# A transformer block with Fourier mixing on one core: row copies from two queues, sums on VectorE, and a new order of outputs and loads

## The chip, the core and the metric

The kernel runs on one core of a Trainium2 chip. The core has five engines with instruction queues of their own: TensorE (PE) for matmuls, VectorE (DVE), ScalarE (ACT) and GpSimd (POOL) for elementwise work, and SyncE (SP), which here only starts transfers. Transfers go through the core's 16 DMA engines; those that SP starts run in a hardware queue (q1 in the profile), those that POOL starts in a software queue (q0). An engine takes its instructions in order, so an instruction that waits holds up everything behind it on the same engine; this is true of SP and POOL when they wait before starting a transfer.

The metric is the device time of one execution in microseconds. The runs of one kernel are compared by their median. Beside it there is one profiled execution, with every instruction's start and length, from which the views below come.

## The reference

```python
y   = x + FNet(x) + MLP(layernorm(x))        # x: 1 x 2048 x 640
# FNet: y = Cs @ (x @ Ch) - Ss @ (x @ Sh), with the DFT matrices of the
#       hidden axis (640 x 640) and of the sequence axis (2048 x 2048)
# MLP:  gelu(h @ w1 + b1) @ w2 + b2, w1: 640 x 1536, w2: 1536 x 640
```

This is its content in short form: a real part of a two-dimensional Fourier transform and a two-layer perceptron on the normalized rows, both added to x. All of it is float32.

## The kernel before

Every float32 product is made of three matmuls of a reduced 32-bit type: high part by high part, high by low, low by high (`product`, L300 to L302; `hidden` has the same in one line, L320). `split` makes the parts: the high part on ACT (L186), the low part on VectorE (L189). One such triple with a 128 x 128 weight and 512 columns is the unit of PE's work.

The 2048 rows are four token blocks of 512 (block 0 to 3), the 1536 hidden columns twelve chunks of 128, and the 640 columns five blocks of 128. The work on PE stands in this order:

- 0 to 92 us: the MLP of block 0. The loop over i splits chunks of w1 and w2 (`prep_w1`, `prep_w2`), starts loads of later chunks (`load_w1`, `load_w2`, on SP), runs `background(i)`, then `hidden(i + 2)` (15 matmuls of L320), `gelu`, `late(i)` and `output(i)` (15 matmuls of L300 to L302). Behind it, `background` and `late` prepare the rows of blocks 1 and 2: layernorm (`ln_scale`, `ln_apply`, L231), then `put_z` and `put_rows`.
- 92 to 211 us: `pair(k)`, k = 0 to 5: blocks 1 and 2 together, two hidden chunks of both at a time, by sums and differences (forms) of their rows, in the manner of Strassen's method. A `window` is a run of products into one bank. In it `term`, `unit` and `split_unit` take the banks over to ACT and VectorE (L340, L463), `put_out(n)` takes n entries off the list `outputs` and runs them as output products, and `beside_pair(k, at)` runs side work at a fixed place: the sums of block 0 (`finish`), the weights of the hidden-axis transform (`turn_w`, `prep_w`), loads.
- 211 to 262 us: the loop over p with the late outputs of block 2. `load_unit(i)` brings a unit back from `gs` in DRAM on SP, `split_unit` splits it, and `between(p)` prepares block 3: layernorm, `put_z`, `put_rows`, transposes, weights, the sums of block 1.
- 262 to 341 us: the MLP of block 3, with the start of the sequence transform's inputs behind it; 342 to 862 us: the sequence transform.

`put_z` (L735) re-lays a block's normalized rows within SBUF, so that a partition holds other rows: 16 copies of 80 KB. It is called for block 2 (`z_b`, from tile r, in `late(1)`), block 1 (into the tile `row`, from `rt`, in `background(3)`; the view names it `row<-rt`), and block 3 (`z<-row`, in `between(3)`). All 48 are started by POOL. `put_rows` (L743) stores the same rows to `xn` in DRAM in four copies of 320 KB; POOL starts them, but for block 2, where SP does, in `background(2)`.

From z the forms are made (`make_forms`): a transpose on VectorE (L259), the high part on ACT (L186), the low part on VectorE (L189). On ACT and VectorE they stand in order with the splits of the weight chunks and the gelus of the loop over i: `make_forms("b", ...)` in `background(4)` and `make_forms("a", ...)` in `background(5)` come in one turn, the split of the chunk for the next `hidden` only in the following turn. `as` and `r` are names of tiles for the parts of w1 and w2.

`finish(t, *es)` takes column block e of the second MLP product of block t out of its bank: ACT adds the bias (L382), VectorE transposes (L384, tile `ot`), and an addition puts it onto x (L386, tile `xo`). That addition runs on POOL for blocks 0 and 2 and on VectorE for block 1. `turn_sum` is the same without the addition. `store_sums` (L918) stores the sums from POOL to `ys` in DRAM. For block 2 the column blocks come as (3), (4, 0) beside the last gelu, and (1, 2) behind it. The build of the sequence transform's sums takes over the place of block 2's `xo`, so its first instruction waits for those stores.

Of the kernel before, what the change touches and what calls it, by code (L numbers as in the profile page):

```python
# [10 lines left out]
F32 = mybir.dt.float32  # L11
# [4 lines left out]
P = 128  # L16
Q = 4
B = 32
# [8 lines left out]
def kernel(  # L27
# [45 lines left out]
    nc = tc.nc  # L73
# [657 lines left out]
    def put_z(z, rows):  # L731

        for a in range(NC):
            for q in range(Q):
                nc.gpsimd.dma_start(  # L735
                    z[q * B : (q + 1) * B].rearrange("r (c a) d -> r a c d", a=NC)[:, a],
                    rows[a * B : (a + 1) * B, :, q * DQ : (q + 1) * DQ],
                )

    def put_rows(t, rows, eng=nc.gpsimd):  # L740

        for a in range(NC):
            eng.dma_start(  # L743
                xn[:, t * B : (t + 1) * B].rearrange("(c a) r d -> a r c d", a=NC)[a], rows[a * B : (a + 1) * B]
            )

    def background(i):

        if i == 0:
            for c in range(NC):  # L750
                ln_apply(c)
            put_rows(0, row_places)
            A["rows_a"] = rows_in("rt2")
            for c in range(NC, 2 * NC):
                load_x(c, home=A["rows_a"])
            ln_stats(8)
            ln_stats(9)
        if i == 2:
            put_rows(2, A["rows_b"], nc.sync)
            ln_stats(4)  # L760
            ln_stats(5)
        if i == 3:
            ln_scale(NC)
            Z["a"] = as_z(row_places)
            for c in range(NC, 2 * NC):
                ln_apply(c)
            put_z(Z["a"], A["rows_a"])
            put_rows(1, A["rows_a"])
        if i == 4:
# [12 lines left out]
        if i == 7:  # L782
            open_place(*PLACES[8])
            make_forms("b", "t10", "t11")
            add(vb, vb, ub, ALU.subtract)
        if i == 8:
            turn_x("t20", "b")
            turn_x("t21", "b")
            add(ua, vb, ua, ALU.subtract)
            add(va, va, vb, ALU.subtract)  # L790
            load_xo(0)

    def late(i):

        if i == 0:
            ln_stats(10)
            ln_stats(11)
        if i == 1:
            ln_scale(NC)
            Z["b"] = zo_tile("z_b")  # L800
            for c in range(2 * NC, 3 * NC):
                ln_apply(c)
            put_z(Z["b"], A["rows_b"])
        if i == 2:
            ln_stats(6)
            ln_stats(7)
# [94 lines left out]
    def keep(g, a):  # L901
        nc.gpsimd.dma_start(gs[g % NF], a)

    def finish(t, *es, home=None, eng=nc.gpsimd):

        for e in es:
            add_block(xo[t], e, oacc[t][e], f"ot{t}_{e}", eng, bias=b2c[:, e : e + 1], **(home or {}))

    def turn_sum(t, e):
        nc.scalar.activation(oacc[t][e], oacc[t][e], AF.Identity, bias=b2c[:, e : e + 1])  # L910
        yt = mr.tile([P, TB], F32, tag="ab", bufs=2, name=f"ot{t}_{e}")
        nc.vector.transpose(yt, oacc[t][e])
        return yt

    def store_sums(t, *ks):
        for k in ks or range(len(YCOLS)):
# [7 lines left out]
    def beside_pair(k, at):  # L924
# [43 lines left out]
        if k == LASTK and at == 2:  # L968
            for i in range(3):
                load_unit(i)  # L970
        if k == LASTK and at == 4:
            for i in range(6, 8):
                load_unit(i)
            load_x(14)
            load_x(15)
            load_xo(1, place("xab2", (P, NB, DQ), F32))

    units = {}
# [7 lines left out]
    def pair(k):  # L986
# [4 lines left out]
        u = term(a1, x_)  # L991
        window(y_, "A", 2, "va", True, ("A", 4, "oa0"))
        make_pieces(k + 1, *(("Bh", "Ah") if k else ("Ah",)))
        beside_pair(k, 2)
        put_out(0 if k else 5)
        u = unit(a1, y_, u, u)
        make_pieces(k + 1, *(("Al", "Bl") if k else ("Al",)))
        window(z_, "D", 2, "t1", True, (b, 2, "ob0"))
        zc = mr.tile([P, TB], F32, tag="zt", bufs=2, name=f"zc{k}") if k else early.tile([P, TB], F32, tag="w2r", bufs=3, name="zc0")
# [26 lines left out]
        if not k:  # L1026
            make_pieces(1, "Dh", "Dl", "Ch", "Cl")
        beside_pair(k, 4)
        outputs.extend((g, e) for g in (a1, a2) for e in range(ND))

    def between(p):

        if p == 0:
            ln_stats(12)
            ln_stats(13)
        if p == 1:
            held = [turn_sum(1, e) for e in (3, 4)]
            A["held"] = held
            ln_stats(14)
        if p == 2:  # L1040
            ln_stats(15)
        if p == 3:
            ln_scale(NC)
            Z["z"] = zo_tile("z3")
            for c in range(3 * NC, 4 * NC):
                ln_apply(c)
            put_z(Z["z"], row_places)
            put_rows(3, row_places)
            new_xt(3)
        if p == 4:  # L1050
            for e, yt in zip((3, 4), A["held"]):
                d = xo[1][:, :, e * B : (e + 1) * B]
                add(d, d, yt.rearrange("p (n i) -> p n i", i=B))
        if 4 <= p < 7:
            finish(1, p - 4, home=in_zt, eng=nc.vector)
        for j in {7: (0,), 8: (1, 2), 9: (3, 4)}.get(p, ()):
            if j == 0:
                transpose_z("x30", Z["z"], 0)
            if j + 1 < ND:
                transpose_z(f"x3{j + 1}", Z["z"], j + 1)  # L1060
            prep_xt(f"x3{j}", j)
        if p == 9:
            load_xo(2)
        if p == 10:
            store_sums(1)
        if p == 11:
            open_place(*PLACES[3])
        if p == 12:
            open_place(*PLACES[2])
        for n in {0: (0,), 4: (1,), 5: (2,), 6: (3,), 7: (4,), 8: (5,), 9: (6,), 10: (7,), 11: (8,), 12: (9, 10), 13: (11,)}.get(p, ()):  # L1070
            prep_w1(AGAIN[n], 2 * NF + n)
            load_w1(2 * NF + 3 + n)

    def fourier_step(i):
        if 2 <= i < 2 + 2 * NK:
# [48 lines left out]
    for p in range(2 + NF):  # L1124
        g = 2 * NF - 2 + p
        if p == NF:
            output(g)
            gelu(g + 2, hidden(g + 2))
        elif p == NF + 1:
            acc = hidden(g + 2)  # L1130
            output(g)

            def fill(k):
                finish(2, *((3,), (4, 0))[k])

            gelu(g + 2, acc, fill)
            finish(2, 1, 2, home=in_zt)
            store_sums(2)
        else:
            output(g, (3, 4, 0, 1, 2) if p == 1 else range(ND))  # L1140
            split_unit(g + 2, units[p])
            if p in (0, 1, 2, 8):
                load_unit(min(8 + p, NF - 1))
        between(p)


# [538 lines left out]
```

## Time and profile before

| | |
|---|---|
| median of 3 runs | 864.52 us (863.22 to 866.62) |
| profiled execution | 864.51 us |
| its span, first to last instruction | 862.5 us |
| mean granted clock of TensorE | 0.998 |
| PE busy | 846.3 us (98%) |
| VectorE busy | 686.9 us (80%) |
| ScalarE busy | 366.7 us (43%) |
| POOL busy | 87.2 us (10%) |
| DMA moved | 166.52 MB, mean 193 GB/s |

Busy time of PE is from the start of a matmul to its modelled end, and matmuls overlap, so 98% leaves open how far PE is from its peak; the count of matmuls in a stretch tells that. In a row of the timeline the first number is the start, the second the length of the group, then engine, line, operation, output and inputs, the count, and in brackets the idle time before the group and what ended it. A DMA row of POOL or SP (`SPq`) is the starting of a transfer, not its flight. A window row gives, for each engine, busy time and the count of instructions, then the granted clock (1.00 is full), the busy share of the DMA engines and what they moved.

### The profile page before, as it was taken

What the parts mean: (1) busy time and instruction counts of PE and PEld (TensorE: products, weight loads), DVE (VectorE), ACT (ScalarE), POOL (GpSimd) and SP (SyncE); (2) the same over time, 40 slices, a digit from 0 to 9 for tenths busy, and PEclk for the clock granted to TensorE, in tenths of its full rate; (3) what the DMA queues carried; (4) which work ended last, traced back from release to release, by engine and by line L of the source; (5) the groups of instructions that cost most, each with busy time, mean ns of one, the idle gap of its engine ahead of it and who ended that gap; (6) DMA issues with size and microseconds to landing.
All of it is one profiled execution on the core that took longest, in us unless ns stands there. A gap on an engine that the chain in (4) does not pass through costs nothing.

```text
span 862.5 us, 10569 instructions
## 1 busy us (share of the span) xinstructions
PE 846.3 (98%) x3711; PEld 696.1 (81%) x3711; DVE 686.9 (80%) x897; ACT 366.7 (43%) x528; POOL 87.2 (10%) x138
## 2 busy tenths in 40 slices
PE   8999999999999999999999999999999999999997
PEld 6877877888877888788888888888888888888885
DVE  6868887875865578988988787998977998886687
ACT  6636565665444456344434333332322422223241
POOL 0360043333334000000000000000000000000000
PEclk9999999999999999999999999999999999999999
DMA  8895546878997893959663659854665879804464
GB/s 231 243 262 158 120 119 205 258 234 289 263 250 182 271 401 92 218 115 231 150 168 87 169 152 313 206 105 129 166 178 178 252 183 231 319 18 177 122 169 106
DMA packets 201252, 166.52 MB, mean 193 GB/s; under 512 B 65744, under 2 KB 172496, under 8 KB 200688
## 3 DMA queue, kind: packets, MB, share of 16 engines
q1 hardware_dynamic: 187552, 138.20, 60.5%
q0 software_dynamic: 8368, 26.75, 9.3%
q10 hardware_dynamic: 5280, 0.92, 0.6%
q8 instruction: 29, 0.48, 0.2%
q14 instruction: 23, 0.19, 0.1%
HBM read 115.75 MB, written 46.14 MB: 188 GB/s over the span
## 4 chain that ended last, share of the span: by engine, by line
PE 74%; DMA 11%; DVE 6%; ACT 3%; SPq 2%; issue 2%; POOL 1%; POOLq 0%; DVEq 0%; ACTq 0%
PE banks L300 24%; PE banks L301 24%; PE banks L302 24%; PE banks L320 3%; DMA w1r<-in_B_w_dram 2%; DMA row<-xn 2%; DMA z_b<-r 2%; DMA xab<-in_A_x_dram 1%; DMA ys<-xo 1%; SPq L278 1%; DVE xab L463 1%; DMA row<-rt 1%; DVE sums L463 1%; POOL xo L386 1%; DVE w1f L189 1%
## 5 line engine op out<-in xcount | busy, mean ns | idle before, releaser
L301 PE MATMUL banks<-as,xab 128*128 128x512 f32 x407 | 158.4, 389 | 0.3 <-DVE as L189 0.3
L186 ACT ACTIVATE as<-r 128x1024 fp32r<-128x1024 f32 x80 | 85.0, 1062 | 173.3 <-PE banks L302 148.5
L300 PE MATMUL banks<-as,xab 128*128 128x512 f32 x407 | 158.3, 389 | 0.0
L302 PE MATMUL banks<-as,xab 128*128 128x512 f32 x407 | 158.3, 389 | 0.0
L189 DVE TENSOR_TENSOR as<-r,as 128x1024 fp32r<-128x1024 f32 x80 | 97.2, 1215 | 38.7 <-ACT as L186 38.7
L301 PEld LDWEIGHTS banks<-as,xab 128*128 128x128 f32 x407 | 76.4, 188 | 16.6 <-DVE as L189 0.8
L300 PEld LDWEIGHTS banks<-as,xab 128*128 128x128 f32 x407 | 76.4, 188 | 15.9
L302 PEld LDWEIGHTS banks<-as,xab 128*128 128x128 f32 x407 | 76.4, 188 | 15.8
L300 PE MATMUL banks<-as,xc 128*128 128x512 f32 x224 | 87.1, 389 | 0.0
L301 PE MATMUL banks<-as,xc 128*128 128x512 f32 x224 | 87.1, 389 | 0.0
L302 PE MATMUL banks<-as,xc 128*128 128x512 f32 x224 | 87.1, 389 | 0.0
L186 ACT ACTIVATE as<-rt 128x1024 fp32r<-128x1024 f32 x32 | 34.0, 1062 | 69.9 <-PE banks L302 57.9
L320 PE MATMUL banks<-xt,xab 128*128 128x512 f32 x240 | 56.7, 390 | 0.0
L320 PEld LDWEIGHTS banks<-xt,xab 128*128 128x128 f32 x240 | 44.9, 188 | 9.5 <-DVE xt L189 0.2
L189 DVE TENSOR_TENSOR hs<-ab,hs 128x512 fp32r<-128x512 f32 x36 | 26.3, 730 | 28.9 <-ACT hs L186 28.4
L302 PEld LDWEIGHTS banks<-as,xc 128*128 128x128 f32 x224 | 42.0, 188 | 8.8
L300 PEld LDWEIGHTS banks<-as,xc 128*128 128x128 f32 x224 | 42.0, 188 | 8.7
L301 PEld LDWEIGHTS banks<-as,xc 128*128 128x128 f32 x224 | 42.0, 188 | 8.7
L300 PE MATMUL banks<-hs,xc 128*128 128x512 f32 x120 | 46.9, 391 | 2.2 <-DVE ot L384 2.2
L301 PE MATMUL banks<-hs,xc 128*128 128x512 f32 x120 | 46.7, 389 | 0.0
L302 PE MATMUL banks<-hs,xc 128*128 128x512 f32 x120 | 46.7, 389 | 0.0
L189 DVE TENSOR_TENSOR as<-rt,as 128x1024 fp32r<-128x1024 f32 x32 | 38.8, 1211 | 5.3 <-ACT as L186 5.3
(228 smaller groups left out, 1662.3 us busy)
## 6 DMA issues: line engine op xcount, KB each, us to landing
raw<-in_A_dft_seq_re_dram SPq DMA_DIRECT2D x64, 256.0 KB, 5.7
raw<-in_A_dft_seq_im_dram SPq DMA_DIRECT2D x64, 256.0 KB, 5.4
w1r<-in_B_w_dram SPq DMA_DIRECT2D x144, 80.0 KB, 3.2
wit<-wst POOLq DMA_DIRECT2D x15, 384.0 KB, 4.0
ws<-wit SPq DMA_DIRECT2D x15, 384.0 KB, 5.5
wit<-wst POOLq DMA_DIRECT2D x20, 256.0 KB, 4.4
forms_ab<-xab SPq DMA_DIRECT2D x4, 1280.0 KB, 7.7
xab<-wit SPq DMA_DIRECT2D x13, 384.0 KB, 4.8
```

The costliest lines, as they stand in the source:

```text
L186: nc.scalar.activation(h, s, AF.Copy)
L189: nc.vector.tensor_tensor(l, s, h.bitcast(F32), op=ALU.subtract)
L278: eng.dma_start(t[q * B : (q + 1) * B], v[q, :, :, f0 : f0 + P])
L300: nc.tensor.matmul(acc, wh, mh, start=first, stop=False, skip_group_check=goes_on)
L301: nc.tensor.matmul(acc, wh, ml, start=False, stop=False, skip_group_check=goes_on)
L302: nc.tensor.matmul(acc, wl, mh, start=False, stop=last, skip_group_check=goes_on)
L320: nc.tensor.matmul(acc, W1[i][:, a, j * P : (j + 1) * P], XT[j][:, b], start=n == 0, stop=n == len(steps) - 1)
L386: eng.tensor_tensor(d, d, yt.rearrange("p (n i) -> p n i", i=B), op=ALU.add)
L463: nc.vector.tensor_tensor(dst, a, b, op=op)
```

## The change

- `put_z` starts its copies from POOL and SP in turn: q = 0 and 2 from POOL, q = 1 and 3 from SP. For each of the three blocks that is 8 and 8.
- `put_rows` is always started by POOL; for block 2 it is called in `late(1)`, right behind `put_z`, no longer in `background(2)`.
- `finish` always adds on VectorE. For block 2 the transposes and the additions are taken apart: `turn_sum` of block 3 in the first gap beside the last gelu; in the second `turn_sum` of 4, 0, 1, the addition of 3, `turn_sum` of 2; the additions of 4, 0, 1, 2 behind the gelu. Their tiles come from two pools, so that none waits for an addition.
- In `pair(k)`, `beside_pair(k, 2)` stands behind `unit(a1, ...)` and no longer ahead of it. It holds `finish(0, 2)` for k = 1 and `prep_w(0, 1)` for k = 2.
- The outputs of pair 0 come as columns 0, 1, 2 of both units, then columns 3, 4 of both.
- In the last pair, x(14) and x(15) are loaded ahead of units 6 and 7; `load_unit(11)` and `load_xo(2)` start behind the w1 load of the same turn.

The number of instructions on PE (matmuls and the rest) and on ACT is unchanged; VectorE has ten more (836 for 826), POOL nine fewer (80 for 89), SP three more (242 for 239).

```diff
@@ put_z, put_rows
-                nc.gpsimd.dma_start(
+                (nc.gpsimd, nc.sync)[q % 2].dma_start(
                     z[q * B : (q + 1) * B].rearrange("r (c a) d -> r a c d", a=NC)[:, a],
                     rows[a * B : (a + 1) * B, :, q * DQ : (q + 1) * DQ],
                 )
-    def put_rows(t, rows, eng=nc.gpsimd):
+    def put_rows(t, rows):
-            eng.dma_start(
+            nc.gpsimd.dma_start(
@@ background
         if i == 2:
-            put_rows(2, A["rows_b"], nc.sync)
@@ late
             put_z(Z["b"], A["rows_b"])
+            put_rows(2, A["rows_b"])
@@ finish, turn_sum
-    def finish(t, *es, home=None, eng=nc.gpsimd):
+    def finish(t, *es, home=None):
-            add_block(xo[t], e, oacc[t][e], f"ot{t}_{e}", eng, bias=b2c[:, e : e + 1], **(home or {}))
+            add_block(xo[t], e, oacc[t][e], f"ot{t}_{e}", nc.vector, bias=b2c[:, e : e + 1], **(home or {}))
-    def turn_sum(t, e):
+    def turn_sum(t, e, home=mr, tag="ab"):
-        yt = mr.tile([P, TB], F32, tag="ab", bufs=2, name=f"ot{t}_{e}")
+        yt = home.tile([P, TB], F32, tag=tag, bufs=2, name=f"ot{t}_{e}")
+    def add_sum(t, e, yt):
+        d = xo[t][:, :, e * B : (e + 1) * B]
+        add(d, d, yt.rearrange("p (n i) -> p n i", i=B))
@@ beside_pair
         if k == LASTK and at == 4:
+            load_x(14)
+            load_x(15)
             for i in range(6, 8):
                 load_unit(i)
-            load_x(14)
-            load_x(15)
@@ pair
-        beside_pair(k, 2)
         put_out(0 if k else 5)
         u = unit(a1, y_, u, u)
+        beside_pair(k, 2)
...
-        outputs.extend((g, e) for g in (a1, a2) for e in range(ND))
+        for es in ((0, 1, 2), (3, 4)) if k == 0 else (range(ND),):
+            outputs.extend((g, e) for g in (a1, a2) for e in es)
@@ between
-            finish(1, p - 4, home=in_zt, eng=nc.vector)
+            finish(1, p - 4, home=in_zt)
-        if p == 9:
-            load_xo(2)
...
+        if p == 8:
+            load_unit(NF - 1)
+        if p == 9:
+            load_xo(2)
@@ the late outputs of block 2
             def fill(k):
-                finish(2, *((3,), (4, 0))[k])
-
+                if k == 0:
+                    kept[3] = turn_sum(2, 3, rows, "yt")
+                else:
+                    kept[4] = turn_sum(2, 4, rows, "yt")
+                    kept[0] = turn_sum(2, 0, **in_zt)
+                    kept[1] = turn_sum(2, 1, **in_zt)
+                    add_sum(2, 3, kept[3])
+                    kept[2] = turn_sum(2, 2, rows, "yt")
             gelu(g + 2, acc, fill)
-            finish(2, 1, 2, home=in_zt)
+            for e in (4, 0, 1, 2):
+                add_sum(2, e, kept[e])
             store_sums(2)
...
-            if p in (0, 1, 2, 8):
-                load_unit(min(8 + p, NF - 1))
+            if p < 3:
+                load_unit(8 + p)
```

More of the change, by code (lines that the diff above doesn't have):

```diff
@@ L1051, in between @@
             for e, yt in zip((3, 4), A["held"]):
-                d = xo[1][:, :, e * B : (e + 1) * B]
-                add(d, d, yt.rearrange("p (n i) -> p n i", i=B))
+                add_sum(1, e, yt)
         if 4 <= p < 7:
-            finish(1, p - 4, home=in_zt, eng=nc.vector)
+            finish(1, p - 4, home=in_zt)
         for j in {7: (0,), 8: (1, 2), 9: (3, 4)}.get(p, ()):
@@ L1133, in fill @@
             def fill(k):
[L1134 removed]
+                if k == 0:
[6 more added lines that the diff above has]
+                    kept[2] = turn_sum(2, 2, rows, "yt")
+            kept = {}
             gelu(g + 2, acc, fill)
[L1137 removed]
+            for e in (4, 0, 1, 2):
+                add_sum(2, e, kept[e])
             store_sums(2)
```

## The prediction

> **What bounds the kernel now.** I read the page first, then busy time in 20-us stretches, then PE's waits, then the timelines around each wait. In the stretches the columns are the window, its length, busy time and count of PE, weight loads, VectorE (DVE), ScalarE (ACT) and GpSimd (POOL), the granted clock, the DMA share and GB/s.
>
> The page:
>
> ```profile
> span 862.5 us, 10569 instructions
> ...
> PE 846.3 (98%) x3711; PEld 696.1 (81%) x3711; DVE 686.9 (80%) x897; ACT 366.7 (43%) x528; POOL 87.2 (10%) x138
> ```
>
> The stretches:
>
> ```profile
> 40.00:60.00 20.00, 20.00 (x90) 16.57 (x89) 13.02 (x29) 6.51 (x10) 13.74 (x26) 1.00 1.04 272
> 60.00:80.00 20.00, 17.80 (x68) 13.33 (x67) 15.90 (x24) 11.06 (x19) 3.87 (x8) 0.91 0.65 187
> 120.00:140.00 20.00, 18.09 (x79) 14.33 (x78) 14.58 (x27) 10.23 (x22) 9.03 (x11) 1.00 0.67 181
> 140.00:160.00 20.00, 18.66 (x82) 14.86 (x81) 17.97 (x42) 13.39 (x30) 8.48 (x15) 1.00 0.70 232
> 200.00:220.00 20.00, 20.00 (x90) 16.57 (x89) 12.61 (x31) 9.57 (x21) 5.71 (x10) 1.00 0.85 296
> 240.00:260.00 20.00, 19.82 (x86) 15.75 (x85) 12.68 (x19) 10.01 (x16) 4.58 (x6) 1.00 0.94 247
> 260.00:280.00 20.00, 19.55 (x86) 15.83 (x85) 11.00 (x12) 9.71 (x16) 10.66 (x8) 1.00 0.71 178
> 340.00:360.00 20.00, 19.66 (x87) 15.96 (x86) 18.57 (x23) 9.92 (x15) 0.00 (x0) 1.00 1.21 223
> ```
>
> PE is busy 98% of the span. In 40:60 and 200:220 it is full: 90 matmuls in 20 us, 0.222 us each. What a stretch lacks of 20.00 can be won, not more: 2.20 us in 60:80, 1.91 in 120:140, 1.34 in 140:160, 0.18, 0.45 and 0.34 in the last three. Besides, 60:80 has a clock of 0.91, which makes busy time long. PE's own instructions stay as they are, so the change can win only there.
>
> PE's waits (in total, times, longest):
>
> ```profile
> PE banks L300 <- DVE ot L384: 2.2, 2, 1.7
> PE banks L320 <- ACT as L186: 1.9, 2, 1.6
> ...
> PE banks L300 <- ACT zc L186: 1.6, 2, 1.3
> ```
>
> PE's timeline at 60-72 us:
>
> ```profile
> 62.14 5.70 PE L320 MATMUL banks<-xt,as 128*128 128x512 f32 x15 [1.57 <-ACT as L186]
> ...
> 71.62 1.59 PE L320 MATMUL banks<-xt,as 128*128 128x512 f32 x4 [0.37 <-ACT as L186]
> ```
>
> PE's timeline in pair 1:
>
> ```profile
> 124.85 0.50 PE L300 MATMUL banks<-hs,xc 128*128 128x512 f32 x1 [1.70 <-DVE ot L384]
> ```
>
> A stretch of 2 us:
>
> ```profile
> 64.00:66.00 2.00, 2.00 (x6) 1.57 (x5) 0.00 (x0) 0.00 (x0) 1.70 (x4) 0.50 0.81 203
> ```
>
> The waits lie in those stretches. At 60–72 us PE waits 1.57 and 0.37 us for `as`, the parts of a w1 chunk. The 15 matmuls of hidden(8) from 62.14 then take 5.70 us instead of some 3.5 (14 x 0.222 and the end of the last), because the clock is 0.50 at 64:66: 2.2 us. Together the place costs 1.57 + 0.37 + 2.2 = 4.1 us; without it hidden(9) would start at 71.62 - 4.1 = 67.5.
>
> Why `as` is late: ScalarE takes its work in order, and ahead of the chunk's high part stand the forms of z.
>
> ACT's timeline:
>
> ```profile
> 66.93 1.22 ACT L186 ACTIVATE xab<-ztua 128x512 fp32r<-128x512 f32 x2 [4.21 <-DVE ztua L259]
> ...
> 70.85 0.72 ACT L186 ACTIVATE as<-w1r 128x640 fp32r<-128x640 f32 x1
> ```
>
> VectorE's timeline:
>
> ```profile
> 66.18 1.30 DVE L259 STREAM_TRANSPOSE ztua<-row 128x512 f32<-128x512 f32 x2 [2.51 <-DMA row<-rt]
> ```
>
> POOL's timeline:
>
> ```profile
> 50.91 1.64 POOL L735 DMA_DIRECT2D row<-rt  x3 [1.53 <-DMA z_b<-r]
> 53.30 1.63 POOL L735 DMA_DIRECT2D row<-rt  x3 [0.75 <-DMA z_b<-r]
> 56.24 3.80 POOL L735 DMA_DIRECT2D row<-rt  x7 [1.31 <-DMA z_b<-r]
> 60.84 0.55 POOL L735 DMA_DIRECT2D row<-rt  x1 [0.80 <-DMA row<-rt]
> 62.32 0.55 POOL L735 DMA_DIRECT2D row<-rt  x1 [0.93 <-DMA row<-rt]
> 63.10 0.55 POOL L735 DMA_DIRECT2D row<-rt  x1 [0.23 <-DMA row<-rt]
> 64.30 2.18 POOL L743 DMA_DIRECT2D xn<-rt  x4 [0.64 <-DMA row<-rt]
> ```
>
> The chain of waits:
>
> ```profile
> 63.10 2.70 DMA row<-rt
> ```
>
> POOL issues the 16 copies of the second z (row<-rt) from 50.91 to 63.65, waiting for landings of its own earlier copies. The chain of waits has the last landing at 65.8, VectorE transposes at 66.18, ScalarE makes the forms from 66.93, and only behind them `as` for hidden(9) at 70.85. So as(9) is ready 5.74 us after that landing (71.58), and hidden(9) starts at 71.62. The wait of 1.57 us before hidden(8) stands likewise behind the forms of the first z (z_b).
>
> **The change, part by part.**
>
> *Copies from two queues.* The 48 row copies (three z of 16) go alternately to POOL and SP, so 24 leave POOL. The four row stores of block 2 go from SP to POOL, behind z_b's eight there. On SP eight copies of z_b come ahead of w1(8), and eight of row<-rt ahead of w1(10) and w2(8); all wait for the layernorm's rows, so these weights wait with them. w1(8) is needed for hidden(8) near 61, some 15 us later: nothing. w1(10) comes from 54.97 to some 58–60, needed near 74: nothing, unless the second z is late. The first z need be only 1.57 us earlier for hidden(8) to run without a wait; POOL's waits on z_b's landings (1.53 + 0.75 + 1.31) alone are longer, so I let that wait and its clock drop go. But that only moves the stall: hidden(9) still needs as(9). The gain of the place is how much earlier the second z lands than 65.84, at most 4.1 us.
>
> Bounds of that landing. Below: POOL's waits for its own landings inside the 16 issues are 0.75 + 1.31 + 0.80 + 0.93 + 0.23 = 4.0 us; with two queues none remain, which gives 61.8. Above: the four block 2 stores (1280 KB) now stand on POOL's queue before row<-rt, and the four xn<-rt come beside SP's half.
>
> SP's timeline:
>
> ```profile
> 43.55 3.50 SPq L743 DMA_DIRECT2D xn<-r  x4
> ...
> 54.97 1.92 SPq L278 DMA_DIRECT2D w1r<-in_B_w_dram  x4
> ```
>
> At the 203 GB/s of 64:66 another 1280 KB in front are 6.3 us, at the 272 of 40:60 they are 4.7: the landing at 70.5 to 72.1. Against it, SP's w1 and w2 chunks that were issued from 54.97 on (w1(10), w2(8), part of w1(11), about 960 KB) now come behind row<-rt, some 3.5 us at 272 GB/s, which gives 67.0 and, with the stores early in flight, up to 70.5 as the end of the range. I take 63.0, nearer the lower end: the rows that end the landing are POOL's waits for itself, with the engines at 0.81 in 64:66, not full. This is -2.8 us, and PE waits 68.7 - 67.5 = 1.2 us there. Whether such a wait halves the clock is open: 1.57 us at 62.14 did, 1.70 us at 124.85 did not (1.00 in 120:140). I charge nothing and keep +2.2 for the range.
>
> The Trainium skill, "DMA: Bandwidth & Descriptors", section "Issuing engines are not separate DMA queues", speaks against this part: copies started from several engines end up on the same 16 DMA engines, and only the time to start them is saved. By it the landing would stay at 65.8 or later, the place would gain nothing, and the sum would be 863.5. The share of 1.04 in 40:60 agrees with it; POOL's waits at issue are the room that the rule leaves.
>
> *Additions on VectorE.* Ten additions leave POOL.
>
> The additions (line 386; min/median/max in ns):
>
> ```profile
> L386 POOL TENSOR_TENSOR xo<-xo,ot x10: 1284/1297/1868, 115.9 to 274.1; 128x512 f32<-128x512 f32 x10
> ...
> L386 DVE TENSOR_TENSOR xab<-xab,ot x3: 692/693/693, 231.7 to 237.1; 128x512 f32<-128x512 f32 x3
> ```
>
> VectorE's timeline in pair 1:
>
> ```profile
> 114.40 0.82 DVE L189 TENSOR_TENSOR w1f<-w1r,w1f 128x640 fp32r<-128x640 f32 x1
> ...
> 118.78 2.87 DVE L189 TENSOR_TENSOR w1f<-w1r,w1f 128x640 fp32r<-128x640 f32 x2
> ...
> 127.34 2.26 DVE L189 TENSOR_TENSOR w1f<-w1r,w1f 128x640 fp32r<-128x640 f32 x1
> 129.53 0.67 DVE L463 TENSOR_TENSOR zc<-zc,banks 128x512 f32<-128x512 f32 x1
> ```
>
> in pair 2:
>
> ```profile
> 151.16 0.68 DVE L463 TENSOR_TENSOR zc<-zc,banks 128x512 f32<-128x512 f32 x1
> ```
>
> On POOL one takes 1297 ns, on VectorE 693. While POOL adds, VectorE's L189 takes 2.87 us for two and 2.26 for one instead of the 0.82 of 114.40: some 2.7 us lost. The five additions of block 0 on VectorE cost 5 x 0.69 = 3.5. Nearly equal, so VectorE comes to zc (129.53) at the same time or up to 0.8 later.
>
> *finish behind the unit, outputs regrouped (pairs 1 and 2).* The wait at 124.85 (1.70 us, third output's bank held by transposition L384) goes, as finish(0,2) no longer stands before it in the way it did, and the 1.3 us for ACT zc in 140:160 goes, because prep_w(0,1) comes behind. What is late next: the window t4 needs zc, made by VectorE, which has no idle time before 129.53 in pair 1 nor before 151.16 in pair 2. PE arrives earlier and waits there instead. I take +0.3 for both, with bounds -3.2 (what 120:140 and 140:160 lack: 1.91 + 1.34) and +2.1 (three additions ahead of zc at 0.69, and none of the lost time regained).
>
> *Third z (block 3).*
>
> POOL's timeline, third z:
>
> ```profile
> 234.63 4.34 POOL L735 DMA_DIRECT2D z<-row  x8 [1.56 <-DMA z<-row]
> ```
>
> PE's timeline, late outputs:
>
> ```profile
> 272.43 0.50 PE L300 MATMUL banks<-hs,xc 128*128 128x512 f32 x1 [0.45 <-DVE ot L384]
> ```
>
> VectorE's, there:
>
> ```profile
> 270.62 1.12 DVE L189 TENSOR_TENSOR hs<-ab,hs 128x512 fp32r<-128x512 f32 x1
> ```
>
> POOL issues 8 copies, waits 1.56 us, issues 8 more; with two queues the last starts some 4 us earlier, x(14) and x(15) come earlier too. PE has 0.18 us missing in 240:260 as idle and 86 matmuls instead of 90, so -0.5, at most 4 x 0.222 = -0.9; later weights come behind the copies, which can give it back: 0 is the other end.
>
> *Block 2's sums in the last outputs.* PE's 0.45 us at 272.43 waits for a transposition, which waited for POOL's sums; VectorE's hs beside them takes 1.12. Transposes first, additions after the gelu: the wait goes, -0.5; 0 if VectorE is late. The stores of block 2 follow as much earlier and the later stretch 340:360 may regain its 0.34: -0.3.
>
> *Loads in another order.* load_unit(11) behind the w1 load, load_xo(2) behind it too, x(14), x(15) ahead of two units: nothing. The cover is PE's queue in 200:220, full; if a unit is late there, PE waits as long as it is late.
>
> Sum: -2.8 + 0.3 - 0.5 - 0.5 - 0.3 = -3.8 (all but the first: -1.0). The profiled execution took 864.51 us (862.5 of span and 2.0 around it), the median of the runs is 864.52: no correction. That gives 860.7 us.
>
> **The rivals.**
>
> *Pairs 1 and 2 gain too* (VectorE is not the bound there). For it: the named waits end on ACT and on a transposition, not on zc's row. Against: VectorE has no idle time in the rows before 129.53. It gives 860.7 - 0.3 - 3.2 = 857.2.
>
> *Bandwidth decides* (the change doesn't bring the copies earlier). For it: the engines' share in 40:60 is 1.04. Against: 0.81 in 64:66. The second z lands between 65 and 67, PE waits 3 to 5 us at 67.5 in one piece, and the clock is halved then: at 65.84 it is 864.5 + 2.2 - 1.0 = 865.7, in all 864.9 to 866.9. This is what the rule of the Trainium skill on issuing engines would bring.
>
> *Slower: the second z is held up behind the rows of block 2.* These 1280 KB stand on POOL's queue before its half of row<-rt, and SP's half alone makes no form. At 70.5 it gives 864.5 + 4.7 + 2.2 - 1.0 = 870.4. It decides from a landing at 68.9 on, where 3.1 + 2.2 - 1.0 = 4.3 over 864.5 is 868.8. Against it: in the trace these stores are in flight from 43.55 on as well, only on the other queue.
>
> **How the numbers follow.** A measurement of this kernel tells about 0.5% from no change (its runs lie within 863.22 to 866.62), so faster is below 860.2 and slower above 868.8. Forecast (landing 62 to 65, the rest as summed: 859.7 to 862.7, and 1 us more to both sides by the smaller terms): 0.40, of it 0.18 below 860.2. Pairs gain too: 0.25, all below. Bandwidth: 0.15, all within. Held up: 0.20. Faster 0.18 + 0.25 = 0.43, same 0.22 + 0.15 = 0.37, slower 0.20. The range goes from 856.4, the pairs' rival with a landing near 62, to 870.4, the held-up landing at its bound.
>
> **What would show it.** The last row<-rt landing near 63 and hidden(9) starting under 70 (right), or over 72 (wrong). Clock in 60:72 at 1.00, or a half clock after 67. In pairs 1 and 2: no waits for a transposition near 124 nor for ACT's zc in 140:160, and a new one before t4 at 131 and 152, or none (then the second case). In 260:280: 89 matmuls and no wait for a transposition. Wrong altogether it would be if a weight chunk, x or a unit behind SP's copies came late, in a wait of PE that is not in the rows of before.

## The result, and the profile after

The changed kernel takes 871.96 us (median of 5 runs, 870.49 to 873.73) against 864.52 for the kernel before: a ratio of 1.0084, with a 95% interval of 1.0062 to 1.0105. It is slower by some 7.4 us. The prediction was 860.7 us, with a range of 856.4 to 870.4. The profiled execution has a span of 870.2 us, 7.7 more than before. The profile counts 20 more transfers started by SP (598 for 578) and 20 fewer by POOL (101 for 121): 24 row copies moved over, four stores moved back.

The stretches of 20 us in the changed kernel, with the columns as before:

```profile
60.00:80.00 20.00, 14.33 (x58) 11.22 (x57) 12.03 (x18) 8.01 (x13) 0.00 (x0) 0.91 0.58 167
120.00:140.00 20.00, 17.89 (x79) 14.15 (x77) 14.80 (x28) 10.91 (x21) 5.53 (x7) 1.00 0.59 151
140.00:160.00 20.00, 18.36 (x81) 14.91 (x80) 17.15 (x43) 12.09 (x30) 7.91 (x14) 1.00 0.73 244
240.00:260.00 20.00, 16.96 (x63) 13.13 (x62) 11.72 (x19) 7.79 (x14) 1.70 (x2) 0.83 0.72 196
260.00:280.00 20.00, 20.00 (x90) 16.58 (x89) 9.03 (x14) 10.65 (x16) 0.00 (x0) 1.00 0.72 173
340.00:360.00 20.00, 20.00 (x90) 16.58 (x89) 18.41 (x24) 10.12 (x17) 0.00 (x0) 1.00 0.88 163
```

The two stretches that should have gained are the ones that lost. In 60:80 the count of matmuls falls from 68 to 58, in 240:260 from 86 to 63 at a clock of 0.83. 260:280 and 340:360 are full now, as forecast. PE's waits, in total, times and longest:

```profile
PE banks L320 <- ACT as L186: 5.7, 1, 5.7
PE banks L300 <- DVE zc L463: 3.0, 2, 1.6
PE banks L300 <- ACT hs L186: 2.9, 1, 2.9
```

The 1.57 and 0.37 us for `as` have become a single wait of 5.67 us. Pairs 1 and 2 wait 3.0 us for zc and 0.7 for a transposition, where they waited 1.6 for zc's high part and 1.7 for a transposition. The 2.89 us for `hs` are new, near 250. The rows of those places, from PE's timeline and in stretches of 2 us:

```profile
72.48 5.14 PE L320 MATMUL banks<-xt,as 128*128 128x512 f32 x15 [5.67 <-ACT as L186]
```

```profile
122.53 0.50 PE L300 MATMUL banks<-hs,xc 128*128 128x512 f32 x1 [0.71 <-DVE ot L384]
...
133.07 0.50 PE L300 MATMUL banks<-as,w1f 128*128 128x512 f32 x1 [1.40 <-DVE zc L463]
```

```profile
250.38 0.79 PE L300 MATMUL banks<-hs,r 128*128 128x512 f32 x1 [2.89 <-ACT hs L186]
```

```profile
72.00:74.00 2.00, 1.52 (x4) 1.06 (x5) 2.00 (x4) 1.06 (x2) 0.00 (x0) 0.53 0.06 22
...
252.00:254.00 2.00, 2.00 (x6) 1.57 (x5) 1.97 (x4) 2.00 (x4) 0.00 (x0) 0.50 0.57 145
```

Behind both long waits the clock is halved: 15 matmuls take 5.14 us from 72.48, where an undisturbed `hidden` takes 3.56, and from 250 to 256 the clock is 0.50.

The account of the 7.7 us goes by the start of the same matmul in both kernels. At 12 us the changed kernel is 0.55 us ahead. Behind hidden(9) it is 1.90 us late, so the place at 60 to 76 costs 2.45 us more than before. Pairs 1 and 2 add 0.24 (their waits add up to 0.5 more than before), the place near 250 adds 5.5, 260:280 wins 0.8 and 340:360 wins 0.7. The stretch behind PE's last matmul is 1.1 us longer, and 0.3 come up elsewhere in the sequence transform. The runs do not connect these two, or the start, with the change.

In the kernel before, the place at 60 to 72 cost more than the prediction's 4.1 us, and less of it was the clock. hidden(9) took 4.10 us there at a clock of 1.00, because the low part of `as` came from VectorE only at 72.43:

```profile
71.62 4.10 PE L320 MATMUL banks<-xt,as 128*128 128x512 f32 x15 [0.37 <-ACT as L186]
```

The low part for hidden(8) came as late (at 62.95, for a start at 62.14). So of its 5.70 us some 1.6 are the half clock, an estimate from these two rows, and not 2.2.

Where the second z was lost stands in the queues of POOL and SP:

```profile
47.54 3.80 POOL L735 DMA_DIRECT2D row<-rt  x7 [1.66 <-DVE rt L231]
52.43 0.55 POOL L735 DMA_DIRECT2D row<-rt  x1 [1.09 <-DMA xn<-r]
54.62 2.17 POOL L743 DMA_DIRECT2D xn<-rt  x4 [1.64 <-DMA row<-rt]
```

```profile
45.76 5.58 SPq L278 DMA_DIRECT2D w1r<-in_B_w_dram  x4
...
52.20 2.88 SPq L278 DMA_DIRECT2D w1r<-in_B_w_dram  x4
...
56.15 8.58 SPq L735 DMA_DIRECT2D row<-rt  x8
```

```profile
67.06 1.30 DVE L259 STREAM_TRANSPOSE ztua<-row 128x512 f32<-128x512 f32 x2 [7.31 <-DMA w1r<-in_B_w_dram]
```

POOL has its half of row<-rt issued by 53.0. SP's half is behind the loads of w1(8), w2(6), w1(9) and w2(7) in SP's order. It starts at 56.15 and takes 8.58 us for eight copies. POOL's half has landed by 58.0, the last of SP's at 66.25, and VectorE begins on that z at 67.06, not at 66.18.

Near 250, ACT makes `hs` behind the split of a w1 chunk, and that chunk comes late. Before, POOL's stores and SP's loads stood so:

```profile
238.96 2.18 POOL L743 DMA_DIRECT2D xn<-row  x4
```

```profile
233.13 17.07 SPq L278 DMA_DIRECT2D w1r<-in_B_w_dram  x16
```

In the changed kernel POOL's stores of the rows begin at 234.76 and those of the sums at 237.51, and SP's loads stand behind its eight copies:

```profile
235.89 1.63 POOL L743 DMA_DIRECT2D xn<-row  x3 [0.58 <-DMA z<-row]
237.51 1.17 POOL L923 DMA_DIRECT2D ys<-xab  x1
```

```profile
237.45 18.85 SPq L278 DMA_DIRECT2D w1r<-in_B_w_dram  x20
```

```profile
249.07 0.74 ACT L186 ACTIVATE as<-w1r 128x640 fp32r<-128x640 f32 x1 [2.66 <-DMA w1r<-in_B_w_dram]
```

### The profile page after: what moved, and what is told of

Read it like the earlier page. It is cut to its first block, busy times and chain, and to the rows that moved or that the text cites. A ratio compares the mean times of both kernels' runs of the same rounds, so it can differ in the third digit from the quotient of the medians.

```text
span 870.2 us, 10596 instructions
## 1 busy us (share of the span) xinstructions
PE 848.1 (97%) x3711; PEld 698.9 (80%) x3711; DVE 687.5 (79%) x907; ACT 367.5 (42%) x528; POOL 62.5 (7%) x108
## 4 chain that ended last, share of the span: by engine, by line
PE 83%; DMA 6%; DVE 6%; SPq 3%; ACT 1%; issue 1%; DVEq 0%; ACTq 0%
PE banks L300 26%; PE banks L301 26%; PE banks L302 26%; PE banks L320 6%; DMA w1r<-in_B_w_dram 2%; DMA w2r<-in_B_w_dram 1%; DMA xab<-in_A_x_dram 1%; SPq L735 1%; SPq L278 1%; DVE ot L384 1%; DVE xab L189 1%; DVE hs L189 1%; DVE w1f L189 1%; DMA row<-in_A_x_dram 0%; DVE w1r L463 0%
```

## The experiments

All ratios are to the kernel before, timed beside each kernel on the same chip. The runs of before scatter between 862 and 872 us, so that differences under 0.2% between two kernels that did not share a chip say little, and parts are compared by their rows. In the edits `put_z` gets its two engines as an argument, where it needs it.

### The second z from POOL alone

```diff
-            put_z(Z["a"], A["rows_a"])
+            put_z(Z["a"], A["rows_a"], (nc.gpsimd,) * 2)
```

> The changed kernel, with the 16 copies of the second z (row<-rt) issued from POOL alone; z_b and z3 stay split. Theory (order of the queue): SP's half of the second z is late because it stands on SP behind the loads of w1(9) and w2(7) and is issued from 56.15 to 64.7, while POOL's half is issued by 53.0. From POOL alone the last landing comes near 62, the wait of 5.67 us before hidden(9) goes, and the time falls by 3 to 6 us, to 866 to 869. Rival (bandwidth): the same bytes are under way, the last landing stays at 65 or later, a wait of 3 us or more stays before hidden(9), and the time stays within 871 to 873. The loss in 240:260 should not move by either.

Measured: 1.0035 (1.0013 to 1.0057), some 4 us less than the whole change. The z comes earlier, though not by as much as I expected, and a wait of 3.27 us stays, with the clock at 0.83 in 60:80. Neither theory was right in full: SP's place in the queue was part of the delay, but all from POOL the last copy does not land at 62 either, but at 64.4. The place near 250 did not gain (a wait of 3.97 us).

```profile
64.55 1.31 DVE L259 STREAM_TRANSPOSE ztua<-row 128x512 f32<-128x512 f32 x2 [4.35 <-DMA xn<-rt]
```

```profile
69.98 6.58 PE L320 MATMUL banks<-xt,as 128*128 128x512 f32 x15 [3.27 <-ACT as L186]
```

The z is 1.6 us earlier than in the kernel before (64.55 against 66.18), and yet PE stands longer in one piece, and 15 matmuls take 6.58 us: here the two short waits of before had cost 1.5 us less than the one long wait.

### The third z from POOL alone

```diff
-            put_z(Z["z"], row_places)
+            put_z(Z["z"], row_places, (nc.gpsimd,) * 2)
```

> The changed kernel, with the 16 copies of the third z (z<-row) issued from POOL alone. Theory: SP's eight copies delay the w1 chunks queued behind them; without them the wait of 2.89 us at 250.4 and the half clock behind it go, and the time falls by 4 to 5.5 us, to 866.5 to 868. Rival: the loads of x(14), x(15), units and xo in their new order cause that wait; then 240:260 keeps its clock of 0.83 and the time stays within 871 to 873. The wait before hidden(9) stays at 5 to 6 us by either.

Measured: 1.0017 (0.9998 to 1.0036), 867.33 us, as expected. No wait for `hs`'s high part is left, and 240:260 is as before.

```profile
60.00:80.00 20.00, 13.17 (x47) 10.16 (x46) 11.54 (x18) 8.19 (x14) 0.00 (x0) 0.74 0.66 185
240.00:260.00 20.00, 19.84 (x87) 15.86 (x86) 14.92 (x24) 7.76 (x13) 9.26 (x14) 1.00 0.94 255
```

So the split of the third z, and not the loads in their new order, makes the loss near 250. 60:80 keeps its own (47 matmuls, clock 0.74, a wait of 6.83 us).

### All copies from POOL

```diff
-                (nc.gpsimd, nc.sync)[q % 2].dma_start(
+                nc.gpsimd.dma_start(
```

> The changed kernel with all 48 row copies issued from POOL, so that of the change there remain the stores of block 2's rows on POOL, the additions on VectorE, the outputs' order and the loads' order. If the split alone makes the change slow, this is as fast as the kernel before or faster by the 1 us that 260:280 and 340:360 win: 862 to 865. If the stores of block 2's rows on POOL ahead of the second z hold it up (the rival that I had put on the slower side), the second z lands after 66 and it takes 867 or more.

Measured: 1.0027 (1.0007 to 1.0046). It is not as fast as before: 60:80 has a wait of 6.07 us. POOL's queue shows why:

```profile
51.69 0.55 POOL L743 DMA_DIRECT2D xn<-r  x1 [0.23 <-DMA z_b<-r]
53.73 2.18 POOL L735 DMA_DIRECT2D row<-rt  x4 [1.48 <-DMA z_b<-r]
56.64 0.55 POOL L735 DMA_DIRECT2D row<-rt  x1 [0.73 <-DMA xn<-r]
...
59.27 4.90 POOL L735 DMA_DIRECT2D row<-rt  x9 [0.34 <-DMA xn<-r]
```

The four stores of block 2 stand in front of row<-rt, whose copies then wait for them (`DMA xn<-r`), and the last of which is started at 63.6. That is the rival of the slower side, on the path where nothing is split.

### Only the split

```diff
-                nc.gpsimd.dma_start(
+                (nc.gpsimd, nc.sync)[q % 2].dma_start(
```

> The kernel before, with nothing changed but that the 48 row copies go alternately to POOL and SP. If the split is the cause by itself, it loses what the whole change loses or 1 us more, 871 to 874, with the waits before hidden(9) and near 250 both there. If the split costs only together with the stores of block 2's rows on POOL or with the loads in another order, it stays under 868.

Measured: 1.0099 (1.0059 to 1.0138), 875.81 us, a little more than expected. The split makes the kernel slow without any of the other edits, with waits of 8.39 us before hidden(9) and 4.69 near 250. SP's half of the second z is issued still later than in the whole change, since SP also has the stores of block 2:

```profile
48.63 4.59 SPq L743 DMA_DIRECT2D xn<-r  x4
53.32 8.90 SPq L278 DMA_DIRECT2D w1r<-in_B_w_dram  x4
...
63.33 5.14 SPq L735 DMA_DIRECT2D row<-rt  x8
```

### Only the first z split

```diff
-            put_z(Z["a"], A["rows_a"])
+            put_z(Z["a"], A["rows_a"], (nc.gpsimd,) * 2)
-            put_z(Z["z"], row_places)
+            put_z(Z["z"], row_places, (nc.gpsimd,) * 2)
```

> The changed kernel with the second and the third z issued from POOL alone; only z_b is split. If the two losses are separate, the gains of the two runs before add: 871.96 - 4.2 (second z) - 5.8 (third z), taken against before 0.9965 to 1.000 of it, 862 to 865.5. The wait before hidden(9) should be the 3 us of the run with the second z from POOL, and 240:260 should be full. If they don't add (the second z from POOL alone then wins nothing of its own), it takes 866 to 868.

Measured: 0.9943 (0.9928 to 0.9958), 863.30 us. The gains of the two runs add, by the ratio to more than their sum (0.9943 against 0.9968). The wait before hidden(9) is 3.29 us, and 240:260 is full.

### SP's copies of the second z ahead of the loads

```diff
+        if i == 3:
+            background(i)
         if i + 6 < NF + 3:
             load_w1(i + 6)
         load_w2(i + 4)
-        background(i)
+        if i != 3:
+            background(i)
```

with the third z from POOL alone.

> The changed kernel with the third z from POOL alone (as in that run, 1.0017 of before), and on SP the eight copies of the second z ahead of the loads of w1(9) and w2(7) and no longer behind them. Theory (place in SP's queue): SP's half is then issued from about 48 on beside POOL's half, the last landing comes before 61, the wait before hidden(9) goes whole with its half clock, 6.8 + 3 us, and the time falls below the kernel before, to 856 to 861. Rival (bandwidth): the copies share the engines with the stores of block 2's rows, the last landing is not before 64, and the time is 863 or more. A further outcome: w1(9), now late, takes its place in a wait for as.

Measured: 0.9931 (0.9910 to 0.9952), 862.29 us. Against the run without this edit that is 0.9% by the ratios, on another chip. Against the run of the next section, which was timed beside it and whose edit has no effect (866.76 us), it is 0.5%. The z lands between the two expectations.

```profile
45.21 5.79 SPq L278 DMA_DIRECT2D w1r<-in_B_w_dram  x4
...
51.61 9.69 SPq L735 DMA_DIRECT2D row<-rt  x8
```

```profile
63.30 1.31 DVE L259 STREAM_TRANSPOSE ztua<-row 128x512 f32<-128x512 f32 x2 [5.45 <-DMA w1r<-in_B_w_dram]
```

Ahead of w1(9), SP begins at 51.61 instead of 56 to 58, so the place in the queue does count. But it takes 9.69 us for eight copies. In the two later runs with these same edits and another change in the pairs it is 9.93 and 10.62. So a second cause stretches SP's issue. The wait before hidden(9) is 1.73 us in this profile, but 4.27 and 4.07 in those two, so how much the place in the queue is worth by itself stays uncertain.

### Block 1's stores later, from POOL

```diff
             put_z(Z["a"], A["rows_a"])
-            put_rows(1, A["rows_a"])
...
             make_forms("a", "ua0", "ua1", "va0")
+            put_rows(1, A["rows_a"])
```

with the third z from POOL alone.

> The changed kernel with the third z from POOL alone, and the four stores xn<-rt behind the next turn's forms, so that POOL does not start them while SP issues its half of the second z. Theory (SP's issue is stretched by POOL's stores in flight, 8.2 to 8.6 us for eight copies instead of 5): the issue takes 5 to 6 us, the second z lands 2 to 4 us earlier, and the time falls by 2 to 5 us from 867.3. Rival: the stretch comes from SP's own loads in flight; the issue stays over 7.5 us and the time at 866 to 868.5.

Measured: 1.0001 (0.9979 to 1.0023), with SP's issue at 8.34 us. This run decides nothing: POOL has nothing to do between the two places, so its stores started at 54.50 as before.

### None of the moves

```diff
-                (nc.gpsimd, nc.sync)[q % 2].dma_start(
+                nc.gpsimd.dma_start(
...
         if i == 2:
+            put_rows(2, A["rows_b"], nc.sync)
...
             put_z(Z["b"], A["rows_b"])
-            put_rows(2, A["rows_b"])
```

> The changed kernel with all row copies from POOL and the stores of block 2's rows on SP at their old place, so that of the change only the additions on VectorE, the outputs' order and the loads' order are left. From the offsets in the traces these lose 0.2 us in pairs 1 and 2 and win 1.0 us behind 260: 0.5 to 1.2 us under before, ratio 0.9985 to 0.9995, and the waits at 60 to 72 are those of before (1.6 and 0.4 us). If the stores on POOL are not what made the run with all copies on POOL slow, it stays at 1.002 to 1.003.

Measured: 0.9957 (0.9940 to 0.9973), 864.11 us. By the ratio it is more than I expected, but before had a median of 867.34 there; by its span, 862.5, it equals the profiled execution of before. Its waits at 60 to 72 are 2.10 and 1.74 us, longer than expected, but without a half clock behind them. What is left of the change does no harm, and the moves carry the loss.

### Block 1's stores from SP

```diff
-            put_rows(1, A["rows_a"])
...
+            put_rows(1, A["rows_a"], nc.sync)
             new_forms(3, "t1")
```

on top of the run with SP's copies ahead of the loads; the stores now stand in `background(6)`, behind the load of w1(12).

> The run with SP's copies ahead of the loads, and besides the four stores xn<-rt of block 1's rows issued by SP in turn 6, behind w1(12), and no longer by POOL at 52. (In the run meant to hold these stores back they had started at 54.5 all the same, since POOL has nothing to do in between.) Theory: in that run SP took 9.69 us to issue eight copies because POOL's four stores of 320 KB were in flight beside them; without them the issue takes 5 to 6.5 us, the second z lands by 61, the wait of 1.73 us and the half clock behind it go, and it takes 857.5 to 860.5. Rival: SP's own loads (w1(8), w2(6)) or the stores of block 2 stretch the issue; then it stays over 8 us, and the time at 861 to 863.5.

Measured: 0.9939 (0.9920 to 0.9959), 859.72 us, with no wait of PE left between 40 and 100 us. The ratio is no better than that of the run it starts from (0.9931). But the two runs of the next section, which were timed beside it and have the same edits up to 92 us except this one, take 863.40 and 864.44 us. SP's timeline, and VectorE's:

```profile
54.10 5.22 SPq L735 DMA_DIRECT2D row<-rt  x8
...
69.87 3.97 SPq L743 DMA_DIRECT2D xn<-rt  x4
```

```profile
61.33 1.31 DVE L259 STREAM_TRANSPOSE ztua<-row 128x512 f32<-128x512 f32 x2 [0.81 <-DMA row<-rt]
```

```profile
60.00:80.00 20.00, 20.00 (x89) 16.33 (x88) 18.17 (x27) 13.17 (x22) 0.00 (x0) 1.00 0.81 233
```

Eight copies take 5.22 us, as in the theory, and VectorE begins at 61.33. Beside SP's copies the edit takes away nothing but POOL's four stores, so these in flight stretched SP's issue. The other runs agree: without these stores, in four profiles, eight copies that begin between 51.0 and 54.1 take 5.15 to 6.40 us; with them, in three, eight copies that begin between 51.6 and 55.1 take 9.69 to 10.62. In the run with only the split POOL had started them at 52.6 to 57.1, and SP's copies came from 63.33 on and took 5.14 us. The four w1 loads of 53.32 there took 8.90; they met POOL's stores and SP's own of block 2.

### The additions, and the order in the pairs

```diff
-            add_block(..., f"ot{t}_{e}", nc.vector, ...)
+            add_block(..., f"ot{t}_{e}", nc.gpsimd if t == 0 else nc.vector, ...)
```

> The run with SP's copies ahead of the loads, with the five additions of block 0 back on POOL. By the prediction's sum (2.7 us of VectorE won, 3.5 spent) pairs 1 and 2 stay within 0.8 us: ratio to before within 0.001 of that run's 0.9931, 862 to 863. If VectorE's slow L189 beside POOL's additions weighs more, the wait before the window t4 grows by 1 to 3 us and so does the time; if the additions themselves hold VectorE up, that wait of 1.4 us shrinks by up to 0.8.

```diff
+        beside_pair(k, 2)
         put_out(0 if k else 5)
         u = unit(a1, y_, u, u)
-        beside_pair(k, 2)
...
-        for es in ((0, 1, 2), (3, 4)) if k == 0 else (range(ND),):
+        for es in (range(ND),):
```

> The run with SP's copies ahead of the loads, with the side work of pairs 1 and 2 back ahead of the unit and the outputs of pair 0 in their old order. If VectorE bounds those pairs, the waits for a transposition (1.7) and for zc's high part (1.3) come back, the waits before t4 (3.0 in total) go, and the time stays within 0.5 us of that run. If the new order wins by itself, the time rises by 1 us or more.

Measured: 0.9970 (0.9951 to 0.9990) and 0.9986 (0.9969 to 1.0003). Both times lie above the run that they start from, but for a reason ahead of the pairs: the second z came later in both profiles (waits of 4.27 and 4.07 us before hidden(9), not 1.73), although these edits act only from 92 us on. What makes it scatter so is not shown. So the totals say nothing on the pairs; the rows do. With the additions on POOL the wait of 0.71 us for a transposition is gone, and the waits for zc stay, at 3.2 in sum; with the old order the waits are 2.6 us for zc's high part and 0.8 for transpositions, 3.4 in all against 3.7.

The additions were then tried where the stage ahead is quiet, on the run with block 1's stores from SP:

> The run with block 1's stores from SP (0.9939 of before, 859.72), with the five additions of block 0 back on POOL. In the trace of the earlier run with that edit pairs 1 and 2 won 0.6 us against before, while with the additions on VectorE they lose 0.3: 0.9 us less here, ratio 0.9925 to 0.9935, about 858.8. If that difference came from the stage before, it stays at 0.994.

Measured, in 5 rounds: 0.9903 (0.9884 to 0.9922), 857.70 us. The waits in pairs 1 and 2 are 1.51 and 1.64 us, without the 0.71. This is the fastest kernel of the study, 0.97% under before and some 1.7% under the change, which was timed on another occasion; the gain over the run that it starts from is more than expected, though the intervals touch.

```profile
125.12 0.50 PE L300 MATMUL banks<-as,w1f 128*128 128x512 f32 x1 [1.51 <-DVE zc L463]
```

### The third z again

The split of the third z on top of the run with block 1's stores from SP; and the same with block 3's stores and block 1's sums issued by SP:

```diff
-            put_rows(3, row_places)
...
         if p == 9:
+            put_rows(3, row_places, nc.sync)
             load_xo(2)
...
-        if p == 10:
-            store_sums(1)
         if p == 11:
+            store_sums(1, eng=nc.sync)
```

> The run with block 1's stores from SP, with the third z split again as in the change. Theory (POOL, free 4 us earlier, starts its stores xn<-row and ys<-xab earlier, and while they are in flight SP takes 1.2 to 2.4 us to issue one w1 load in place of 0.43): the wait of 3 to 4 us near 250 and its half clock come back whatever the stages ahead do, plus 4.5 to 6 us: 864 to 866, and the slow issues stand at the first w1 loads behind the copies.

> As the run with the third z split again, and the stores xn<-row issued by SP behind the w1 loads of turn 9, ys<-xab of block 1 by SP in turn 11. Theory (stores of POOL in flight slow SP's issues): w1 loads behind the copies are issued at 0.5 us each or less than 1 us, the wait near 250 goes, and it takes 858 to 861. Rival (place in the queue: eight copies ahead of the w1 loads are what makes them late): the wait near 250 stays over 2 us and the time at 863 to 866.

Measured: 0.9976 (0.9957 to 0.9994) and 1.0004 (0.9987 to 1.0021). The first brings the loss back where the stage before is quiet: a wait of 3.37 us and 63 matmuls in 240:260. In the second that place is full; SP's timelines of the two, and the stretches of the second:

```profile
224.96 6.13 SPq L735 DMA_DIRECT2D z<-row  x8
231.19 18.93 SPq L278 DMA_DIRECT2D w1r<-in_B_w_dram  x20
```

```profile
223.83 5.60 SPq L735 DMA_DIRECT2D z<-row  x8
229.53 12.10 SPq L278 DMA_DIRECT2D w1r<-in_B_w_dram  x20
...
255.49 7.57 SPq L923 DMA_DIRECT2D ys<-xab  x3
```

```profile
240.00:260.00 20.00, 20.00 (x90) 16.57 (x89) 7.35 (x11) 6.91 (x10) 0.00 (x0) 1.00 0.87 203
260.00:280.00 20.00, 14.84 (x57) 11.74 (x56) 9.16 (x15) 7.87 (x13) 3.41 (x3) 0.83 0.68 165
```

The same twenty w1 loads behind the same eight copies take 18.93 us from the first to the last with POOL's stores in flight (waits for free tiles included) and 12.10 without them; the first six take 9.9 and 3.5. The wait near 250 goes. So the place in the queue, the rival, does not make that wait by itself for this z.

The total did not follow, and that expectation missed. SP starts the sums `ys` from 255.49 to 263.06, and ACT may write the parts of a w1 chunk into the tile `xab` only when the last of them has landed:

```profile
266.69 0.74 ACT L186 ACTIVATE xab<-w1r 128x640 fp32r<-128x640 f32 x1 [10.67 <-DMA ys<-xab]
```

Behind it stand a bias and a transposition, for which PE waits 5.16 us near 269 instead.

## Why the prediction was wrong

**Copies from two queues, second z (-2.8): wrong, +2.5.** The step that failed is the lower bound, "with two queues none remain, which gives 61.8", and the choice of 63.0 near it. I let the waits of POOL's queue go and put no queue's waits in their place. I had written that SP's copies come ahead of w1(10) and w2(8), and priced that, but not that they come behind w1(8), w2(6), w1(9) and w2(7); SP came to its half at 56.15, when POOL had been done for three us, and the last copy landed at 66.25. Two prices were missing. One is the place in SP's queue: ahead of the loads, SP's copies begin 4.5 us earlier (51.61 against 56.15). The other is POOL's stores: without them beside it, SP takes 4.5 us less for eight copies (5.22 against 9.69). I had named "the four xn<-rt come beside SP's half" and put no price on them.

**The clock: wrong.** "I charge nothing" for a wait in one piece; it was halved, for 1.6 us here, up to 3.0 in the run with the second z from POOL. The 2.2 us that I gave it in the kernel before were too many: 4.10 us of a `hidden` at full clock show that the late low part of `as` takes 0.5 of them.

**The first z: right.** hidden(8) starts without a wait in the changed kernel; and, as said, that only moved the stall.

**Third z (-0.5): wrong, +5.5.** I took "0 is the other end" for what later weights could give back. POOL was free 4 us earlier, its stores xn<-row and ys<-xab started as much earlier, and they met the first w1 loads behind the copies. Before, they met loads from 244.98 on, for a chunk that ACT takes only at 254.46. The step that failed is the other end of 0: it has no price for a w1 chunk that comes late enough to stop PE. This is a gain that turned into an earlier collision; the last two runs show it.

**Pairs 1 and 2 (+0.3): right.** The two waits named went, and new ones of 1.40 and 1.64 us stand before t4 for zc, +0.5 in the sum of the waits and +0.24 by the same matmul. The rival in which these pairs gain is out. The sign of the additions alone was not in the sum: on POOL they are better by the 0.71 us of a wait for a transposition.

**Block 2's sums (-0.5) and 340:360 (-0.3): right.** Both stretches are full, and they win 0.8 and 0.7. **The loads' order (0): right**, as the run with the third z from POOL shows: 240:260 has 87 matmuls there.

**The rivals.** "Held up" had the right side and, for the kernel with all copies from POOL, the right mechanism. In the changed kernel itself block 2's stores did not hold POOL's half back, it was issued by 53.0. "Bandwidth decides" described this place best: a landing between 65 and 67, one long wait, a half clock. Its total of 865.7 lacks the third z. Its cause, that the copies share the engines with the other transfers, is there in part: in the changed kernel the DMA engines are 0.93 to 1.02 busy from 54 to 62 us, while SP is slow, and 0.54 from 64 on, when it is not. But the place in SP's queue counts besides.

```profile
60.00:62.00 2.00, 2.00 (x11) 1.65 (x10) 0.00 (x0) 0.00 (x0) 0.00 (x0) 1.00 1.02 372
64.00:66.00 2.00, 2.00 (x11) 1.65 (x10) 0.00 (x0) 0.00 (x0) 0.00 (x0) 1.00 0.54 123
```

The rule of the Trainium skill that I had weighed ("DMA: Bandwidth & Descriptors", "Issuing engines are not separate DMA queues") says that all queues end on the same engines; it was the better guide than POOL's rows, since the second z landed no earlier in the change. The run with block 1's stores from SP has the same 16 copies from two queues and is 4.9 us earlier at VectorE than before (61.33 against 66.18). How much of that the second queue brings is not shown: the run also has SP's loads behind the copies and block 1's stores later, and no run has these two with all copies from POOL.

## What to carry to other kernels

Before you spread transfers over a second queue, write down what stands ahead of them on that queue, and what the first queue will start earlier once it has been relieved; both are prices, and here the two places lost 2.5 and 5.5 us against hoped gains of 2.8 and 0.5. Urgent small copies belong ahead of loads that are not yet due, and large stores nobody waits for belong behind them, on a queue where they really come later. A long wait in one piece can cost more than its length: here up to 3.0 us of half clock came on top.

## What the runs showed of the hardware

Large stores in flight make SP's own issuing slow, not only the flight: in the runs of this study the eight copies of the second z, 80 KB each, take SP 5.1 to 6.4 us without POOL's four stores of 320 KB beside them (5.22 in the row above), and 8.2 to 10.6 with them (9.69). The copies of the first z tell less: they take 6.3 to 8.2 us, and 6.75 in the run with only the split, where no such store is beside them. The stores need not be POOL's. In the kernel before, SP's four w1 loads behind its own stores of block 2 take 5.93 us, and the next four, at 54.97, take 1.92:

```profile
47.75 5.93 SPq L278 DMA_DIRECT2D w1r<-in_B_w_dram  x4
```

Whether SP waits for room in the engines, which are 0.93 to 1.02 busy in that stretch of the changed kernel, or for something else is not shown.

Behind the first 20 us, all waits of PE of 2.9 us or more in these profiles were followed by a clock of 0.50. Between 1.3 and 2.1 us it went both ways: 1.57 us in the kernel before and 1.73 in the run with SP's copies ahead of the loads halved it, 1.70 at 124.85 in the kernel before, and 2.10 and 1.74 us in the run with none of the moves, left it at 1.00:

```profile
60.00:80.00 20.00, 15.91 (x67) 11.91 (x66) 16.14 (x24) 11.11 (x18) 4.77 (x9) 1.00 0.67 181
```

The Trainium skill, "TensorE: Matmul & The Clock Gate", "What's actually happening", has a window of about 3.4 us that runs freely, after which an idle array is throttled. That a wait of this length can cost nothing or 1.6 us of half clock agrees with a freely running window; that 1.57 us were enough does not agree with a window that must be idle in full.
